# Block outputs formed transposed in PSUM, weight remainders by matmul, and another order of steps, in a fused linear-attention and mixture kernel on one core

## The chip, the cores and the metric

The kernel runs on one NeuronCore of a Trainium2 chip, as one launch. The core has five engines with queues of their own: TensorE (PE, with its weight loads PEld), VectorE (DVE), ScalarE (ACT), GpSimd (POOL) and SyncE (SP), whose queue issues all DMAs here. The metric is the device time of a run in microseconds; before the change it is 583.61 us, the median of 3 runs (582.99 to 583.75).

## What is computed

```python
for t in range(S):                       # B, H, S, D = 4, 8, 768, 48
    cur = einsum('bhd,bhe->bhde', u * k[t], v[t])
    y[t] = einsum('bhd,bhde->bhe', r[t], state + cur)
    state = w[t][..., None] * state + einsum('bhd,bhe->bhde', k[t], v[t])
x = y as 3072 tokens of 384              # heads side by side
h = x @ w_in; x = (h * cos(h)) @ w_out   # 384 -> 2048 -> 384, float64 weights
logits = x @ phi                         # 32 slots, 4 for each of 8 experts
slot_in = softmax(logits over tokens).T @ x
slot_out[e] = relu(slot_in[e] @ w1[e]) @ w2[e]     # 384 -> 1024 -> 384
out = softmax(logits over slots) @ slot_out
```

## The kernel before

**Attention.** The 3072 tokens are cut into 24 blocks of 128; a block is two chunks of 64 tokens, and heads go in four pairs. A block `j` is a series of short steps, each on one engine: the decays are transposed (`wT`, PE) and copied (`wf`, ACT); two running products are scanned on DVE (`scan` L153, `sp` L161); keys and receptances are transposed and scaled (`kT`, `ks`; `rT`, `L`); the scores of a chunk are formed (`A`) and masked, either on DVE straight from PSUM (`mask` L217) or by an ACT copy and a product on GpSimd (`mc`, `mp` L237), which the first seven blocks use; `U` gives what a chunk adds to the state; `z`, `st` carry the state on DVE and `rz` copies it, with ACT, into the tile `rz`, which already holds the chunk's values. `y` (L285) multiplies the tile `L` (scores and receptances) with `rz`: 16 products with 64 columns of `L` as weights and 48 columns of `rz` moving. The bonus of u is a product of r, u and k on GpSimd (`ru` L166, L167), a sum on DVE (`bo`) and a product with v on GpSimd (`bv` L257). `ya` (L295) adds it to `y` on DVE, from PSUM to SBUF; `xT` (L300) transposes the sum back into PSUM; `xh`, `xl` split it into two float32r parts, the left operand of the next stage.

**Weights.** w_in and w_out come as float64 words, in 8 pieces each, and are cut to float32 with integer operations: `abs` on ACT, then `mx`, `d1`, `d2a`, `d2b` on DVE. The list of steps has other ways for some pieces: `mxp` (the `mx` of L362 on GpSimd) and `d2s` with `d2p` (L383, L388: the shift on DVE, the addition on GpSimd). w_in is split in two float32r parts: `whi` on ACT and `wlo` (L402) on GpSimd. w_out stays float32; phi is multiplied into it by `oT`, `oc`, `om`, `pc`, `pT`, `ps` (L407 to L433).

**Feed-forward.** 12 groups of 256 tokens, each with 8 banks of 2 x 128 hidden columns. A half bank is 9 matmuls (`h`, L454 to L456); then come `turns` (ACT), `rest` (DVE L470), `cos` (ACT L474), `mul` (DVE L478), four transposes (`gT` L486) and a copy (`gc` L491). `l` (L499) takes logits, and `E` (L586) adds the group to the sums for the slots. Softmax statistics go with each group; all but the last use the Silu table, which lies in one set with Sin, the last uses Exp (`s_exp` L535), and the step `tab` loads that set.

**Tail.** When attention's memory is free, `att` loads six expert matrices of 1536 KB, `we` five more into places that w_in and the activations leave, and eight follow behind the last group and as experts are done; these are w1 in rows of 4096 B and w2 in rows of 1536 B (L669).

**Order.** Each engine runs its instructions in the order in which the program lists them, and `HEAD` (L897) is that list, written out: one word for a step, with its block, or group and bank. The transposes, scores and outputs of attention share one ring of three PSUM banks (`tps`).

Of the kernel before, what the change touches and what calls it, by code (L numbers as in the profile page):

```python
# [1055 lines left out]
```

## Time and profile before

| what | value |
|---|---|
| time, median of 3 runs | 583.61 us |
| span of the profiled execution | 579.7 us |
| PE busy | 507.9 us, 88% |
| DVE busy | 472.4 us, 81% |
| ACT busy | 312.8 us, 54% |
| POOL busy | 199.1 us, 34% |

The time of the profiled execution is known by its span, from its first instruction to its last; the 3.9 us to the median of the runs lie around it and are carried as they are. Busy times of engines overlap. A PE that is busy need not be at its peak, since the time of a matmul covers the start of the next ones; how many matmuls pass in a stretch tells more.

### The profile page before, as it was taken

The numbers are of one execution on the slowest core, as the hardware profiler recorded it, in microseconds if no ns is written. First come the engines' busy times: TensorE is split into PE (matmuls) and PEld (weight loads), VectorE is DVE, ScalarE is ACT, GpSimd is POOL, SyncE is SP. The second block draws the span as 40 slices with busy tenths as digits, with TensorE's granted clock in tenths as the row PEclk, the third lists the DMA queues.
The fourth block names the chain that finished last, engine by engine and source line by source line (L and its number), as shares of the span: only waits on it lengthen the run. The fifth ranks groups of instructions, "written<-read, shape, count | busy, mean of one in ns | idle before, by whom it ended". The sixth has DMA issues, their size and how long they took to land.

```text
span 579.7 us, 14183 instructions
## 1 busy us (share of the span) xinstructions
PE 507.9 (88%) x5778; PEld 436.1 (75%) x5778; DVE 472.4 (81%) x857; ACT 312.8 (54%) x655; POOL 199.1 (34%) x194
## 2 busy tenths in 40 slices
PE   2437968978999989999999999999989999998994
PEld 1335748767888969788888987897878979895663
DVE  5998999999898888798788899878979886657422
ACT  3334655665656465465565464654644756566421
POOL 5677865787241323241222231203221130000400
PEclk9957998799999999999999999999999999999997
DMA  9962764553241413330407232044032059568959
GB/s 239 254 168 63 165 163 97 111 135 58 56 83 29 83 29 55 57 69 7 90 19 106 45 63 51 13 71 84 1 63 36 16 218 355 191 218 263 377 176 277
DMA packets 150800, 67.39 MB, mean 116 GB/s; under 512 B 127568, under 2 KB 142928, under 8 KB 150736
## 3 DMA queue, kind: packets, MB, share of 16 engines
q1 hardware_dynamic: 150736, 66.49, 46.1%
q8 instruction: 46, 0.75, 0.6%
q14 instruction: 18, 0.15, 0.1%
HBM read 61.75 MB, written 4.72 MB: 115 GB/s over the span
## 4 chain that ended last, share of the span: by engine, by line
DVE 43%; PE 40%; ACT 7%; issue 5%; DMA 3%; SPq 0%; ACTq 0%; DVEq 0%
PE h L454 6%; PE h L456 6%; PE h L455 6%; DVE qt L153 5%; PE gT L486 4%; DVE pt L161 4%; DVE g L470 4%; DVE g L478 4%; DVE L L184 3%; DVE z L275 3%; DMA we<-in_moe_w_dram 3%; PE l L499 2%; ACT g L474 2%; DVE ao L373 2%; DVE L L224 2%
## 5 line engine op out<-in xcount | busy, mean ns | idle before, releaser
L454 PE MATMUL h<-x,wu 128*128 128x256 f32 x573 | 172.8, 301 | 0.1
L455 PE MATMUL h<-x,wu 128*128 128x256 f32 x573 | 162.5, 284 | 0.0
L456 PE MATMUL h<-x,wu 128*128 128x256 f32 x573 | 162.5, 284 | 0.0
L454 PEld LDWEIGHTS h<-x,wu 128*128 128x128 f32 x573 | 110.4, 193 | 1.0 <-PE wT L138 0.3
L455 PEld LDWEIGHTS h<-x,wu 128*128 128x128 f32 x573 | 110.7, 193 | 0.2
L456 PEld LDWEIGHTS h<-x,wu 128*128 128x128 f32 x573 | 110.3, 192 | 0.0
L474 ACT ACTIVATE g<-g,half_pi 128x512 f32<-128x512 f32 (+1 forms) x97 | 69.6, 718 | 68.1 <-DVE g L470 67.3
L466 ACT ACTIVATE g<-h 128x512 int32<-128x512 f32 x96 | 57.2, 596 | 51.2 <-PE h L456 43.5
L478 DVE TENSOR_TENSOR g<-g,h 128x512 f32<-128x512 f32 x96 | 65.0, 678 | 20.6 <-ACT g L474 19.9
L470 DVE SCALAR_TENSOR_TENSOR g<-g,h 128x512 f32<-128x512 int32 x96 | 64.9, 676 | 19.7 <-ACT g L466 16.7
L257 POOL TENSOR_TENSOR bv<-vz,bo 64x384 f32<-64x384 f32 x48 | 48.2, 1005 | 55.4 <-DVE bo L249 18.4
L491 ACT COPY gt<-gT 128x512 f32<-128x512 f32 x92 | 53.5, 583 | 24.4 <-PE gT L486 16.4
L486 PE MATMUL gT<-cs,g 128*128 128x128 f32 x384 | 59.5, 279 | 4.9 <-DVE g L478 4.8
L190 POOL MEMSET L<- 64x512 f32 x32 | 16.6, 519 | 111.4 <-PE y L291 78.9
L486 PEld LDWEIGHTS gT<-cs,g 128*128 128x128 f32 x384 | 43.3, 141 | 15.3 <-issue 6.1
L166 POOL TENSOR_TENSOR ru<-rn,u_b 128x384 f32<-128x384 f32 x24 | 27.7, 1153 | 72.6 <-DVE bo L249 36.5
L280 ACT COPY rz<-z 64x192 f32<-64x192 f32 x96 | 33.5, 349 | 25.1 <-DVE z L275 24.2
L291 PE MATMUL y<-rz,L 128*64 128x48 f32 x768 | 29.2, 231 | 12.9 <-DVE st_state L283 12.1
L291 PEld LDWEIGHTS y<-rz,L 128*64 128x64 f32 x768 | 26.3, 145 | 16.8 <-issue 14.1
L161 DVE TENSOR_TENSOR_SCAN pt<-wf,ini_f 128x520 f32<-128x520 f32 x24 | 35.3, 1473 | 0.3
L153 DVE TENSOR_TENSOR_SCAN qt<-wf,one_b 128x520 f32<-128x520 f32 x24 | 34.7, 1446 | 0.3
L499 PE MATMUL l<-g,p_sb 128*32 128x256 f32 x384 | 31.0, 393 | 3.6 <-DVE g L478 3.6
(180 smaller groups left out, 942.9 us busy)
## 6 DMA issues: line engine op xcount, KB each, us to landing
we<-in_moe_w_dram SPq DMA_DIRECT2D x16, 1536.0 KB, 9.7
rawi<-in_moe_w_in_dram SPq DMA_DIRECT2D x7, 768.0 KB, 4.8
wn<-in_w_dram SPq DMA_DIRECT2D x24, 192.0 KB, 3.5
kn<-in_k_dram SPq DMA_DIRECT2D x24, 192.0 KB, 4.2
rn<-in_r_dram SPq DMA_DIRECT2D x24, 192.0 KB, 3.6
vz<-in_v_dram SPq DMA_DIRECT2D x48, 96.0 KB, 3.3
rz<-in_v_dram SPq DMA_DIRECT2D x96, 48.0 KB, 2.5
out_dram<-ob SPq DMA_DIRECT2D x17, 256.0 KB, 3.8
```

Source lines behind the costliest of these rows:

```text
L153: nc.vector.tensor_tensor_scan(qt[:, n:0:-1], wf[:, n:0:-1], one_b[:, n:0:-1], 0.0, ALU.mult, ALU.add)
L161: nc.vector.tensor_tensor_scan(pt, wf[:, 0:NS * SEG], ini_f, 0.0, ALU.mult, ALU.add)
L291: nc.tensor.matmul(ps[64 * c:64 * c + 64, 2 * p + a, :], lhsT=L[:, a, 2 * p + c, :], rhs=rz[:, c, p, a, :], start=True, stop=True)
L454: nc.tensor.matmul(hp, lhsT=wh, rhs=xh[:, c, :], start=(c == 0), stop=False)
L455: nc.tensor.matmul(hp, lhsT=wh, rhs=xl[:, c, :], start=False, stop=False)
L456: nc.tensor.matmul(hp, lhsT=wl, rhs=xh[:, c, :], start=False, stop=(c == KD - 1))
L466: nc.scalar.activation(gt.bitcast(I32), hp, AF.Copy, bias=0.25, scale=1.0 / TWO_PI)
L470: nc.vector.scalar_tensor_tensor(out=gt, in0=gt.bitcast(I32), scalar=-TWO_PI, in1=hp, op0=ALU.mult, op1=ALU.add)
L474: nc.scalar.activation(gt, gt, AF.Sin, bias=half_pi[:, 0:1])
L478: nc.vector.tensor_tensor(out=gt, in0=gt, in1=hp, op=ALU.mult)
L486: nc.tensor.transpose(ps[:, tt, mm, :], gt[:, mm, tt * 128:(tt + 1) * 128], ident)
L491: (nc.vector.tensor_copy if NBK * g + i >= ATT and i in (1, 2) else nc.scalar.copy)(t, pend.pop(("gT", g, i)))
```

## The change

`y` is formed transposed. The new `e_y` uses 32 columns of `rz` as weights and 64 columns of `L` moving, 32 products for a block instead of 16, into the PSUM layout that `xT` had; `e_yb` adds the bonus to it with three transposing matmuls that accumulate. `ya`, the tile `y` and `xT` are gone. For this the tile of values is padded to 64 columns a head, in two fixed tiles (`rzs`) whose padding GpSimd writes once. The scores `A` of block 8 and later are formed with 64 moving columns instead of 128, and `mask` is two products instead of four. `mc` and `mp`, `mxp`, `d2s` and `d2p` are no longer in the list: all masks, all `mx` and all `d2b` are on DVE. `wlo` gives way to `wn`, two matmuls into PSUM (a times the identity, minus the rounded part times the identity), and `wc`, an ACT copy. `om` has w_out's tile as weights, so `pc` and `pT` go. w2 is loaded in rows of 3072 B, and a transpose in the tail reads every second column to fit. The list `HEAD` is another throughout.

```diff
+    neg = sm_p.tile([128, G], F32R, tag="lg", name="neg", bufs=1)[:, 0:128]      # -identity, by ACT at the start
+    rzs = [nat.tile([128, 2, HP, 2, 64], F32, name=f"rzs{i}") for i in range(2)]
+    RZ = (slice(0, D), slice(64 - D, 64))
...
     def e_A(j):
-        for s in range(NS if j >= WIDE else 0):
-            m, x = slice(64 * (s % 2), 64 * (s % 2) + 64), s - s % 2
-            nc.tensor.matmul(ps[m, x:x + 2, :], lhsT=ks[:, s, :], rhs=L[:, :, s, :], start=True, stop=True)
...
+        for s in range(NS):
+            for a in range(2):
+                k = slice(0, 128) if j >= WIDE else slice(64 * a, 64 * a + 64)
+                nc.tensor.matmul(ps[64 - 64 * a:128 - 64 * a, s, :], lhsT=ks[k, s, :], rhs=L[k, a, s, :], start=True, stop=True)
...
     def e_y(j):
-        for p in range(HP):
-            for a in range(2):
-                for c in range(2):
-                    nc.tensor.matmul(ps[64 * c:64 * c + 64, 2 * p + a, :], lhsT=L[:, a, 2 * p + c, :], rhs=rz[:, c, p, a, :],
-                                     start=True, stop=True)
+        for c in range(2):
+            for a, b in ((0, 0), (0, 1), (1, 0), (1, 1)):
+                for p in range(HP):
+                    o, m = divmod(32 * (3 * p + a + b), 128)
+                    nc.tensor.matmul(ps[m:m + 32, o, c * C:(c + 1) * C], lhsT=rz[:, c, p, a, 32 * b:32 * b + 32], rhs=L[:, a, 2 * p + c, :],
+                                     start=m not in begun, stop=False, skip_group_check=True)
+    def e_yb(j):
+        for c in range(KD):
+            nc.tensor.matmul(pend["xT", j][:, c, :], lhsT=y[:, c * 128:(c + 1) * 128], rhs=ident, is_transpose=True,
+                             start=False, stop=c == KD - 1, skip_group_check=True)
...
+    def e_wn(n, q):
+        nc.tensor.matmul(ps, lhsT=ident, rhs=a[:, k], start=True, stop=False)
+        nc.tensor.matmul(ps, lhsT=neg, rhs=hi[:, k], start=False, stop=True)
+    def e_wc(n, q):
+        nc.scalar.copy(win(n)[2][:, k], pend.pop(("wl", n, q)))
...
-            nc.tensor.matmul(pt_ps[u_][32 * q:32 * q + 32, 0:128], lhsT=phi_sb[:, c, :], rhs=wt_t[m][:, c, :], start=(c == 0), stop=(c == KD - 1))
+            nc.tensor.matmul(pt_ps[0][:, m, :], lhsT=wt_t[m][:, c, :], rhs=phi_sb[:, c, :], start=(c == 0), stop=(c == KD - 1))
...
-                src = w2[idx - NE].rearrange("(c p) f -> p c f", p=128)
+                src = w2[idx - NE].rearrange("(q p c) f -> p q (c f)", q=4, c=2)
```

What the other list does to the queues is seen in the programs' instructions. On DVE, in the first 40 us, where w_out's first pieces (`ao`, `rawo`) are cut: before,

```order
L364 TENSOR_SCALAR ao_249<-ao_249 128x768
L368 TENSOR_SCALAR ao_249<-ao_249 128x768
L273 MEMSET z_0_253 128x192
L373 SCALAR_TENSOR_TENSOR ao_249<-rawo_245,ao_249 128x768
L364 TENSOR_SCALAR ao_256<-ao_256 128x768
L249 TENSOR_REDUCE bo_264<-ru_261 128x8
L386 TENSOR_SCALAR rawo_245<-rawo_245 128x768
L368 TENSOR_SCALAR ao_256<-ao_256 128x768
L373 SCALAR_TENSOR_TENSOR ao_256<-rawo_245,ao_256 128x768
```

and now:

```order
L222 TENSOR_TENSOR L_218<-A_282,cs 64x512 x2
L277 TENSOR_TENSOR st_state<-U_264,z_1_299 128x192
L357 TENSOR_SCALAR ao_260<-ao_260 128x768
L361 TENSOR_SCALAR ao_260<-ao_260 128x768
L199 TENSOR_TENSOR ks_323<-kT_310,qt_197 128x512
L366 SCALAR_TENSOR_TENSOR ao_260<-rawo_238,ao_260 128x768
L374 SCALAR_TENSOR_TENSOR wo_sb<-rawo_238,ao_260 128x768
```

The mask of block 0 (L222) and the last cut (L374) are now DVE's own; the shift alone (L386) is gone.

On POOL, behind the first memsets (`ru` and `bv` are the bonus): before,

```order
L390 TENSOR_TENSOR ai_158<-rawi_152,ai_158 128x768
L404 TENSOR_TENSOR wu_194<-ai_158,wu_194 128x3x256
L404 TENSOR_TENSOR wu_242<-ai_163,wu_242 128x3x256
L166 TENSOR_TENSOR ru_261<-rn_119,u_b 128x384
L167 TENSOR_TENSOR ru_261<-ru_261,kn_121 128x384
L240 TENSOR_TENSOR L_216<-L_216,cs 64x512 x2
L390 TENSOR_TENSOR wo_sb<-rawo_245,ao_249 128x768
L257 TENSOR_TENSOR bv_316<-vz_125,bo_264 64x384 x2
```

and now:

```order
L169 TENSOR_TENSOR ru_240<-rn_117,u_b 128x384
L170 TENSOR_TENSOR ru_240<-ru_240,kn_119 128x384
L251 TENSOR_TENSOR bv_252<-vz_123,bo_250 64x384 x2
L169 TENSOR_TENSOR ru_479<-rn_118,u_b 128x384
L170 TENSOR_TENSOR ru_479<-ru_479,kn_120 128x384
L251 TENSOR_TENSOR bv_498<-vz_124,bo_482 64x384 x2
```

Only the bonus is left on POOL in this stretch.

On ACT, at the last group (`dl`, `al`: its exponentials; `gt`: its transposed activations; `dt`: what `E` needs): before,

```order
L686 ACT_TABLE_LOAD
L686 ACTIVATE half_pi<-half_pi 128x1
L491 COPY gt_5_6922<-gT_5_6885 128x512
L491 COPY gt_6_6937<-gT_6_6932 128x512
L533 COPY dl_115<-lc_6941 32x64 x4
L491 COPY gt_7_6957<-gT_7_6952 128x512
L543 ACTIVATE dl_115,sg_6968<-dl_115,nb_6946 128x64
```

and now:

```order
L530 COPY dl_112<-lc_7335 32x64 x4
L540 ACT_TABLE_LOAD
L540 ACTIVATE dl_112,sg_7362<-dl_112,nb_7340 128x64
L541 ACTIVATE al_7361<-dl_112,nb_7340 128x1
L575 COPY dt_7375<-dT_7373 64x64 x2
L488 COPY gt_7_7394<-gT_7_7352 128x512
L488 COPY gt_6_7396<-gT_6_7378 128x512
```

The load of the Exp set stood ahead of the copies and now stands right before the exponential; `tab` has moved to group 0, where the list now causes three table loads (one for Exp, one back to Sin, one for Silu).

## Rows read from the trace of the kernel before

**Rows 1.** The profile page: busy time; DVE's busy tenths in 40 slices of 14.5 us.
```profile
PE 507.9 (88%) x5778; PEld 436.1 (75%) x5778; DVE 472.4 (81%) x857; ACT 312.8 (54%) x655; POOL 199.1 (34%) x194
DVE  5998999999898888798788899878979886657422
```
**Rows 2.** Stages: start:end, length, busy us and instructions by engine, clock, DMA share, GB/s.
```profile
8.00:128.60 120.60, 84.57 (x867) 71.19 (x867) 117.89 (x145) 59.76 (x111) 86.46 (x52) 0.86 0.64 151
128.60:169.30 40.70, 38.23 (x439) 33.92 (x436) 37.47 (x57) 24.54 (x55) 23.50 (x18) 1.00 0.38 66
169.30:479.00 309.70, 295.82 (x3367) 259.12 (x3365) 266.22 (x542) 176.71 (x376) 78.20 (x94) 1.00 0.30 58
479.00:533.50 54.50, 52.85 (x522) 46.46 (x519) 33.66 (x77) 34.91 (x76) 0.82 (x1) 1.00 0.73 261
```
**Rows 3.** Waits of DVE, 0 to 128.6 us, the longest: us in total, times, longest.
```profile
DVE ai L364 <- ACT ai L360: 6.9, 1, 6.9
```
**Rows 4.** Groups of DVE instructions, 8 to 128.6 us: busy us, mean ns.
```profile
L153 DVE TENSOR_TENSOR_SCAN qt<-wf,one_b 128x520 f32<-128x520 f32 x7 | 13.0, 1860 | 0.0
L275 DVE TENSOR_TENSOR z<-st_state,qt 128x192 f32<-128x192 f32 x11 | 9.8, 893 | 0.1
L297 DVE TENSOR_TENSOR y<-y,bv 128x384 f32<-128x384 f32 x5 | 2.8, 551 | 0.8 <-PE y L291 0.8
```
**Rows 5.** DVE in order of time, 24 to 58 us: start, us.
```profile
26.02 1.50 DVE L368 TENSOR_SCALAR ao<-ao 128x768 int32<-128x768 int32 x1
30.32 0.55 DVE L386 TENSOR_SCALAR rawo<-rawo 128x768 int32<-128x768 int32 x1
51.64 0.34 DVE L275 TENSOR_TENSOR z<-st_state,qt 128x192 f32<-128x192 f32 x1
54.12 0.95 DVE L381 SCALAR_TENSOR_TENSOR ai<-rawi,ai 128x768 int32<-128x768 int32 x1
57.60 1.23 DVE L161 TENSOR_TENSOR_SCAN pt<-wf,ini_f 128x520 f32<-128x520 f32 x1
```
**Rows 6.** Groups of instructions of the whole run, shapes apart.
```profile
L228 DVE TENSOR_TENSOR L<-A,cs 64x512 f32<-64x512 f32 x2 | 1.4, 690 | 0.0
L224 DVE TENSOR_TENSOR L<-A,cs 64x256 f32<-64x256 f32 x64 | 27.0, 422 | 1.1
L686 ACT ACT_TABLE_LOAD x1 | 1.3, 1283 | 0.0
```
**Rows 7.** Groups of POOL instructions, 0 to 128.6 us, shapes apart: busy us, mean ns.
```profile
L240 POOL TENSOR_TENSOR L<-L,cs 64x512 f32<-64x512 f32 x12 | 19.5, 1624 | 1.9 <-ACT L L235 1.1
L404 POOL TENSOR_TENSOR wu<-ai,wu 128x768 fp32r<-128x768 f32 x8 | 15.8, 1983 | 13.3 <-ACT wu L400 13.3
L257 POOL TENSOR_TENSOR bv<-vz,bo 64x384 f32<-64x384 f32 x10 | 13.2, 1319 | 0.4
L166 POOL TENSOR_TENSOR ru<-rn,u_b 128x384 f32<-128x384 f32 x5 | 6.8, 1359 | 0.2
```
**Rows 8.** PE in order of time: start, us to the end of the last one, count.
```profile
201.52 0.28 PE L456 MATMUL h<-x,wu 128*128 128x256 f32 x1
...
202.16 1.14 PE L291 MATMUL y<-rz,L 128*64 128x48 f32 x32
203.23 0.64 PE L499 MATMUL l<-g,p_sb 128*32 128x256 f32 x8
...
210.57 1.09 PE L204 MATMUL A<-L,ks 128*64 128x128 f32 x16 [0.86 <-DVE st_state L283]
...
564.61 1.96 PE L824 MATMUL so<-we,wo_sb 128*32 128x128 f32 x64
```
**Rows 9.** The chain that ended last: the tail's DMA.
```profile
542.03 15.30 DMA we<-in_moe_w_dram
```
**Rows 10.** Two stretches in which only expert matrices load: w1, then w2.
```profile
482.00:494.00 12.00, 12.00 (x110) 11.28 (x110) 7.06 (x17) 6.82 (x14) 0.00 (x0) 1.00 1.02 410
535.00:554.00 19.00, 18.99 (x336) 11.65 (x340) 7.53 (x20) 7.43 (x20) 5.86 (x9) 1.00 1.06 375
```

More of the change, by code (lines that the diff above doesn't have):

```diff
@@ L649, in rwkv_moe_kernel @@
                 nc.gpsimd.memset(t[64 * c:64 * c + 64, :, 1 - c, :], 0.0)
+        for t in rzs:
+            for a in range(2):
+                nc.gpsimd.memset(t[:, :, :, a, 48 - 48 * a:64 - 48 * a], 0.0)
         nc.gpsimd.memset(ini_f, 0.0)
@@ L906 @@
-bo.2 d2b.i.4 wT.3 wf.3 scan.3 bv.2 om.5 oT.7 oc.7 rT.2 L.2 whi.4 lk.3 ru.3 sr.3 om.6 kN.2 om.7 abs.i.3 mx.i.3 wT.4 h.0.0.1 wlo.4
-ksn.2 turns.0.0 sp.3 wf.4 d1.i.3 rest.0.0 kT.3 A.2 ks.3 h.0.1.0 mc.2 mp.2 U.2 d2a.i.3 d2s.i.3 lk.4 kN.3 raw.i.6 lz.2 lw.5 lk.5 lv.3
-rT.3 st.2.0 cos.0.0 mul.0.0 d2p.i.3 z.2.1 abs.i.6 mx.i.6 st.2.1 d1.i.6 d2s.i.6 rz.2.1 d2a.i.6 h.0.1.1 turns.0.1 rest.0.1 rz.2.0
-ksn.3 gT.0.0 h.0.2.0 h.0.2.1 gc.0.0 turns.0.2 whi.3 cos.0.1 pc.1 L.3 y.2 ya.2 z.3.0 scan.4 kT.4 d2p.i.6 whi.6 mul.0.1 wlo.3 lr.5
@@ L910 @@
-lv.4 A.3 mc.3 ks.4 wlo.6 U.3 st.3.0 rest.0.2 z.3.1 bo.3 sr.4 l.0.1 raw.i.5 abs.i.5 st.3.1 raw.i.7 cos.0.2 mul.0.2 sp.4 kN.4 ksn.4
-abs.i.7 mx.i.7 h.0.3.0 h.0.3.1 pT.1 gT.0.2 xT.2 gc.0.2 ps.1 xh.2 mxp.i.5 d1.i.5 lr.4 lz.3 rz.3.0 rz.3.1 d2s.i.7 d2a.i.5 xl.2
-h.0.4.0 rT.4 wT.5 wf.5 gT.0.1 d2b.i.5 mp.3 whi.5 L.4 h.0.4.1 d1.i.7 turns.0.3 rest.0.3 d2a.i.7 lw.6 bv.3 y.3 ya.3 A.4 lz.4 raw.o.4
-wlo.5 d2p.i.7 lw.7 gc.0.1 cos.0.3 z.4.0 mul.0.3 ru.4 raw.o.5 mc.4 U.4 scan.5 st.4.0 turns.0.4 rest.0.4 abs.o.4 sr.5 kT.5 z.4.1 wT.6
@@ L914 @@
-gT.0.3 whi.7 wlo.7 h.0.5.0 h.0.5.1 sp.5 cos.0.4 st.4.1 ks.5 l.0.3 rT.5 mul.0.4 wf.6 turns.0.5 rest.0.5 L.5 kN.5 xT.3 gc.0.3 lv.5
-ksn.5 cos.0.5 gT.0.4 h.0.6.0 mul.0.5 bo.4 scan.6 mxp.o.4 d1.o.4 h.0.6.1 abs.o.5 gc.0.4 xh.3 turns.0.6 xl.3 d2a.o.4 mxp.o.5 d1.o.5
-rz.4.0 rz.4.1 gT.0.5 A.5 gc.0.5 h.0.7.0 h.0.7.1 mc.5 d2b.o.4 oT.9 oT.8 turns.0.7 mp.4 y.4 oc.9 oc.8 d2a.o.5 rest.0.6 cos.0.6 lk.6
-lz.5 d2b.o.5 om.8 om.9 oT.11 bv.4 ya.4 oc.11 mul.0.6 oT.10 oc.10 lr.6 sr.6 mp.5 rest.0.7 cos.0.7 z.5.0 U.5 st.5.0 z.5.1 sp.6 st.5.1
@@ new lines @@
+turns.0.2 wc.1.1 mul.0.0 gT.0.0 om.4 lk.3 kT.3 mask.2 z.2.1 st.2.1 scan.3 ks.3 rest.0.2 whi.4 abs.i.3 mx.i.3 d1.i.3 sr.3 d2a.i.3
+d2b.i.3 sp.3 wn.4.0 kN.3 ksn.3 wn.4.1 h.0.1.0 h.0.1.1 wc.4.0 lw.5 raw.i.6 abs.i.6 lv.4 whi.3 gc.0.0 lk.4 mx.i.6 cos.0.2 wc.4.1
+wn.3.0 oT.7 wc.3.0 rT.3 wn.3.1 raw.i.5 d1.i.6 rz.2.1 oc.7 y.2 wc.3.1 d2a.i.6 turns.0.1 abs.i.5 mul.0.2 L.3 A.3 wT.4 h.0.3.0
+d2b.i.6 wf.4 mx.i.5 d1.i.5 z.3.0 whi.6 mask.3 wn.6.1 ps.0 wc.6.1 rest.0.1 scan.4 yb.2 om.5 cos.0.1 xh.2 kT.4 d2a.i.5 ru.3 lk.5
@@ new lines @@
+st.4.0 z.4.1 st.4.1 rz.4.1 d2b.o.4 y.3 mul.0.4 l.0.3 A.4 yb.3 xh.3 kT.5 ks.5 mask.4 h.0.5.0 xl.3 h.0.5.1 lw.6 lk.6 raw.o.6 rT.5
+mx.o.5 lz.5 d1.o.5 turns.0.5 kN.5 ksn.5 sr.5 rest.0.5 oT.8 gT.0.3 oc.8 oT.9 sp.5 d2a.o.5 gc.0.3 bo.4 oc.9 d2b.o.5 cos.0.5 h.0.7.0
+h.0.7.1 lv.5 bv.5 turns.0.7 wT.6 om.9 wf.6 mul.0.5 gT.0.5 rest.0.7 L.5 oT.11 raw.o.7 U.5 A.5 oc.11 om.11 z.5.0 scan.6 st.5.0
+abs.o.6 mx.o.6 z.5.1 lw.7 abs.o.7 d1.o.6 d2a.o.6 st.5.1 rz.5.1 om.8 cos.0.7 z.6.0 d2b.o.6 mul.0.7 h.0.6.0 h.0.6.1 wT.7 oT.10
@@ new lines @@
+h.1.1.0 h.1.1.1 mask.5 tab turns.0.6 gc.0.5 rest.0.6 gT.0.4 kT.6 cos.0.6 oc.10 sr.6 sp.6 mul.0.6 ks.6 oT.13 oc.13 rz.5.0 om.10
+gc.0.4 ps.2 wf.7 rT.6 mx.o.7 d1.o.7 h.1.0.0 oT.12 oc.12 d2a.o.7 d2b.o.7 close l.0.5 om.13 oT.14 oT.15 om.12 turns.1.1 bv.4 ru.6
+oc.14 oc.15 h.1.0.1 scan.7 om.15 om.14 gT.0.6 rest.1.1 y.5 lz.7 turns.1.0 cos.1.1 rest.1.0 mul.1.1 cos.1.0 mul.1.0 L.6 y.4 ps.3
+l.0.7 A.6 gc.0.6 sum.0 lc.0 sr.7 gT.0.7 h.1.2.0 h.1.2.1 max.0 exp.0 lv.6 mask.6 lw.9 turns.1.2 gc.0.7 xt.0 rest.1.2 cos.1.2
@@ new lines @@
+h.1.7.1 h.2.1.0 h.2.1.1 dc.0 turns.1.7 rest.1.7 A.7 scan.8 U.7 sr.8 sp.8 st.7.0 z.7.1 st.7.1 l.1.5 y.6 cos.1.7 mul.1.7 E.0.0
+rz.7.0 l.1.7 wT.9 gc.1.5 turns.2.1 rest.2.1 cos.2.1 rz.7.1 gT.1.4 gc.1.4 mask.7 zl.8 bv.7 mul.2.1 h.2.0.0 h.2.0.1 turns.2.0 kT.8
+gT.2.1 rest.2.0 cos.2.0 mul.2.0 E.0.1 yb.6 es.0 bo.8 wf.9 gc.2.1 h.2.3.0 rT.8 gT.1.6 L.8 lz.8 ks.8 h.2.3.1 turns.2.3 rest.2.3
+cos.2.3 sum.1 scan.9 h.2.2.0 sr.9 mul.2.3 xh.6 gc.1.6 xl.6 h.2.2.1 y.7 l.2.1 gT.1.7 yb.7 turns.2.2 rest.2.2 kN.8 lc.1 max.1 xh.7
@@ new lines @@
+y.8 turns.2.6 rest.2.6 ks.10 mul.2.7 bv.8 zl.10 E.1.0 E.1.1 cos.2.6 mul.2.6 gc.2.5 l.2.5 l.2.7 sum.2 gT.2.4 es.1 yb.8 rT.10 sp.10
+lk.12 L.10 h.3.1.0 h.3.1.1 turns.3.1 st.9.0 z.9.1 rz.9.1 bo.9 rest.3.1 gc.2.4 lw.11 xh.8 cos.3.1 xl.8 h.3.0.0 lv.10 mul.3.1
+h.3.0.1 A.10 lc.2 wT.11 st.9.1 turns.3.0 rest.3.0 lw.13 mask.10 cos.3.0 mul.3.0 gT.2.6 gc.2.6 max.2 exp.2 xt.2 xr.2 kN.10 h.3.2.0
+h.3.2.1 gT.3.1 lz.10 h.3.3.0 h.3.3.1 l.3.1 gc.3.1 turns.3.2 rest.3.2 wf.11 scan.11 ksn.10 cos.3.2 mul.3.2 y.9 turns.3.3 xd.2
@@ new lines @@
+lv.13 l.3.5 cos.3.7 mul.3.7 ks.12 rz.10.1 y.10 bv.10 gT.3.5 mask.11 cmb.0.2 h.4.0.0 h.4.0.1 bo.12 rest.3.6 gc.3.5 cos.3.6
+turns.4.0 st.11.0 z.11.1 rz.11.1 gT.3.4 rT.12 yb.10 lk.13 xh.10 st.11.1 mul.3.6 rest.4.0 lz.12 lv.12 sp.12 zl.12 gc.3.4 cos.4.0
+h.4.1.0 h.4.1.1 gT.3.7 wT.13 gc.3.7 mul.4.0 h.4.2.0 es.2 L.12 h.4.2.1 xl.10 l.3.7 turns.4.1 rest.4.1 cos.4.1 turns.4.2 cmb.0.3
+mul.4.1 A.12 wf.13 gT.3.6 gc.3.6 sum.3 rest.4.2 cos.4.2 rz.11.0 kN.12 h.4.3.0 ksn.12 mul.4.2 lc.3 scan.13 max.3 gT.4.1 gc.4.1
```

249 lines of the change are left out of this document (110 added, 139 removed).

## The prediction

> **What bounds the kernel now.** I read the page first, then a table of stages, then the waits and groups of the stage that stood out. The page has PE at 88% and DVE at 81%, and its slices show DVE nearly full in the first tenth to quarter of the run [rows 1]. The stages separate the two. The first matmul of group 1 starts at 128.6 us; from 8 us to there DVE is busy 117.9 of 120.6 us and PE only 84.6. From 128.6 to 533.5 us, when the last `E` ends, PE is busy 38.2 + 295.8 + 52.9 = 386.9 of 404.9 us and DVE 337.4 [rows 2]. So DVE sets the end of the head and PE that of the long middle. In the head DVE waits for nothing worth having: 6.9 us for its first piece of w_in [rows 3], and twice 0.8 us.
>
> DVE's head is not all work. There a scan takes 1.86 us on average and `z` 0.89 us [rows 4]; where GpSimd runs nothing beside them the same instructions take 1.23 and 0.34 us, and a simple operation on 768 columns takes 0.55 us instead of 1.50 [rows 5]. Counting every DVE group of the head in that way, mean less the undisturbed time, gives 32 us of stretching: the scans 7 x 0.63 = 4.4, `z` 11 x 0.55 = 6.0, the weight operations and the other scan the rest. GpSimd is busy 86.5 us of that stage [rows 2].
>
> **The head, up to group 1.** I counted the steps ahead of the first bank of group 1 in both lists. DVE gains five masks from PSUM, 2 x 0.69 us each [rows 6]: +6.9; six `d2b` at 0.95 [rows 5]: +5.7; seven `mx` at 0.55: +3.9; one `d1` and one `d2a` of a piece that now comes sooner: +1.5. It loses five `d2s` at 0.55 and five `ya` at 0.55 [rows 4, 5]: -5.5; and one `sp`, one `ks` and one bank's `rest` and `mul` fall behind the mark, less a `bo` and a `z`: -2.6. The net is +9.9 us, from 96 to 106 us undisturbed.
>
> GpSimd loses `mp`, `wlo`, `mxp` and `d2p`, of which the first two alone are 35 us [rows 7]. What stays is six `ru` and five `bv`, 12 instructions of 1.36 and 10 of 1.32 us, 29 us at these prices [rows 7], a third of 86.5; undisturbed they would be about 20 us, a quarter. So the stretching falls from 32 to between 7 and 11 us; I take 9. DVE's sum changes by 9.9 - 23 = -13.1 us. Neighbouring instructions overlap a little (128 us of durations make 118 busy), so this is worth 12.2 us of time. Against it: the remainders of w_in now go PE, ACT, PE through the ring of three banks in which attention's transposes queue, and a table load of 1.28 us [rows 6] stands on ACT twice in group 0, with a third after it. Behind each wait the banks' `cos` and attention's copies. ACT is half idle there [rows 2], so I give back 2 us of a possible 0 to 12. Head: **-10.2 us**.
>
> PE's new work in the head is hidden by DVE: a remainder is two plain matmuls and one float32r matmul's worth of columns. From 256 columns at 0.21 us plain and 0.12 us float32r [rows 8], 512 + 256 columns, the plain ones in two passes, cost 1.6 us, 13 us for 8 pieces. If that cover were gone they would all count. `om` trades 128 moving columns for 128 weight columns: I take nothing, between -6 us and 0. The `wc` copies (16, some 7 us) take the place of the `mc` copies, 6 x 1.16 us.
>
> **The middle, where PE counts.** The output `y` is the term to settle. Each float32 product is two matmuls in the trace, so `y` is 32 now and 64 after. 32 take 1.14 us with a last one of 0.22: 0.029 us each, 0.059 for a pair on two column halves [rows 8]. Where columns bound, a pair of 128 columns (`A`) takes 0.109 and four of 128 (`so`) take 0.107 us [rows 8], 0.85 ns a column whatever the number of tiles. 48 columns would be 0.041, so `y` is held by something else, which fits its weights, 128 columns a pair. After the change four matmuls have 64 moving and again 128 weight columns. The price of four is 0.054 us if columns bind, 0.059 if weights do as now, and 0.107 if no four go faster than the fastest four in the trace. I take 0.059, from the nearest row: 16 x 0.059 = 0.94 us a block, as now. `yb` is three transposes, as `xT` was.
>
> `A` of block 8 and later goes from 8 pairs at 0.109 to 16 at 0.059: about -0.09 us for 16 blocks, -1.4 us. `pT` goes, -0.5. With 13 added, PE's sum grows by 10.9 us, 9.6 of it ahead of the mark. That leaves +1.3 us behind it. Steps I price at 390 us on PE now take 404.9 us there, a ratio of 1.04, so **+1.4 us**. DVE has 15 us less to do there, 19 `ya` and 64 masks of 0.42 turned into 32 of 0.69 [rows 4, 6]; PE binds, so I count 1 us of it, between 0 and 9: **-1 us**.
>
> **The tail.** The Exp table was loaded beside other work; now its 1.28 us [rows 6] stand between the last group's copies and its exponential, and `E` follows: +1.2. The second half of that `E` waits for two copies behind `dt` instead of one: +0.4. The last five expert matrices, 7.9 MB, are in flight from about 533 us and PE waits 15.3 us for the last of them [rows 9]; they flow at 375 GB/s in rows of 1536 B, while w1 came at 410 in rows of 4096 B [rows 10]. Rows of 3072 B lie between: -1.8 to 0, I take -1.7. Tail: **-0.1 us**.
>
> Sum: -10.2 + 1.4 - 1 - 0.1 = -9.9 us. It is made on the profiled span of 579.7 us, giving 569.8; the 3.9 us around the span stay, so the median of 583.6 becomes **573.7 us**.
>
> **Rivals.**
>
> *Narrow matmuls bind (slower).* At 0.107 us for four, `y` costs 1.71 us, +0.77 a block. 20 blocks have their `y` behind the mark, where PE counts: +15.4 us, 589 us with nothing absorbed, some 586 with PE's idle 4% taking some. It decides from 0.09 us for four on, where 20 x 16 x 0.031 us eats the 9.9. For it: no row sustains less than 0.027 us a matmul, and the change asks for 0.015. Against it: at 0.027 the `so` row is explained by its columns alone. The Trainium skill, "TensorE: Matmul & The Clock Gate", Part 1 (the section on 56 ns against 53.3 ns), says that matmuls never start less than about 25 ns apart, however few the columns; by that rule a block's `y` is 1.6 us and the result near 587. The trace respects that figure on average and does not test it, as it has no shorter matmuls on four tiles.
>
> *The head's gain is given back.* DVE takes over work that nothing has to fetch from GpSimd, but each mask now waits on PE, and `y`'s PSUM bank is held until `bv` has come and `xl` is done, with two banks left for the rest. If the waits replace the stretching, the change does not do what it can: 12 us of gain gone is 584, half gone is 578. For it: DVE had only 1.6 us of such waits in the head, so the order was loose where this one may not be. Against it: masks and `d2b` sit several instructions behind their sources in the new queue.
>
> *PE closes up.* PE is idle 18 us in the middle. If fewer DVE steps there bring back half, the result is 565. Against it: most of DVE's waits there are on ACT's part of a bank, which does not change.
>
> **From cases to numbers.** The forecast, 566 to 580, has 0.53; narrow matmuls 0.17, mostly slower; the gain given back 0.18, half of it still faster, the rest about even; PE closing up 0.12. Within 0.2% (1.2 us) is about what a measurement of this kernel can tell from no change. That makes 0.74 faster, 0.06 the same, 0.20 slower. The range takes the forecast, most of PE's case and most of the narrow one: 563 to 587.
>
> **What would show it.** Right: group 1's first `h` near 118 us in the profile, not 128.6; scans near 1.3 us in the head and POOL busy near 25 us there; `y` at about 1 us for 64 matmuls; the stretch from that `h` to the last `E` near 405 us; the wait for w2 with over 390 GB/s. Wrong: a `y` of 1.7 us is the first rival; DVE idle by over 10 us in the head, on PE or ACT, is the second; under 396 us in the middle the third. A table load on the chain in the tail would confirm that term, and one in group 0 that delays DVE would correct my 2 us.

## The result and the profile after

The changed kernel takes 565.54 us, the median of 4 runs (562.68 to 567.16); the kernel before took 583.3 us beside it (581.6 to 583.75). The ratio is 0.970, 95% interval [0.967, 0.973]: 17.8 us faster, where 9.9 were forecast. Its profiled execution is the slowest of the four: 567.16 us, with a span of 565.4. In all executions on record whose time and span are both known the time is 1.7 to 2.1 us above the span, so the 3.9 us that the forecast carried do not all lie around it: 579.7 us is the span of one of the shorter executions of the kernel before, of some 581.6 us. The two profiles are therefore 14.3 us apart and not 17.8.

The busy line, DVE's slices and the shares of the chain that ended last, from the page of the changed kernel:

```profile
PE 516.0 (91%) x6846; PEld 447.6 (79%) x6846; DVE 438.7 (78%) x823; ACT 313.3 (55%) x657; POOL 123.2 (22%) x163
DVE  4998997996778888788887799897897596666413
PE 58%; DVE 27%; ACT 6%; DMA 4%; issue 3%; SPq 0%; DVEq 0%; ACTq 0%
```

The same last line on the page of the kernel before:

```profile
DVE 43%; PE 40%; ACT 7%; issue 5%; DMA 3%; SPq 0%; ACTq 0%; DVEq 0%
```

DVE is less full at the start than in [rows 1], and the chain has passed from DVE to PE. The stages, cut at the same events as in [rows 2] (group 1's first `h` at 123.0 us, group 2's at 161.4, the last `E` ending at 520.5; columns as there):

```profile
8.00:123.00 115.00, 91.67 (x986) 75.57 (x986) 103.37 (x157) 60.02 (x113) 28.82 (x26) 0.91 0.69 157
123.00:161.40 38.40, 38.18 (x463) 35.39 (x464) 28.52 (x50) 25.46 (x52) 4.59 (x5) 0.96 0.38 63
123.00:520.50 397.50, 386.68 (x5263) 345.85 (x5263) 317.24 (x625) 236.18 (x506) 83.69 (x103) 1.00 0.37 88
520.50:565.40 44.90, 36.61 (x594) 25.48 (x594) 16.05 (x38) 14.19 (x34) 5.86 (x9) 0.95 0.81 282
```

| stage | before | after | moved | forecast |
|---|---|---|---|---|
| head, to group 1's first `h` | 128.6 | 123.0 | -5.6 | -10.2 |
| middle, to the end of the last `E` | 404.9 | 397.5 | -7.4 | +2.0 (the middle's +0.4, the tail's +1.6 ahead of `E`) |
| behind it | 46.2 | 44.9 | -1.3 | -1.7 |

In the head DVE is busy 103.4 us instead of 117.9, a little less than the 105.7 that follow from the forecast, but it now idles 11.6 us instead of 2.7. In the middle PE is as busy as before (386.7 against 386.9 us), and its idle time fell from 18.0 to 10.8 us. DVE is busy 20.1 us less there.

Two groups of DVE answer to [rows 4], in the head (busy us, mean ns):

```profile
L156 DVE TENSOR_TENSOR_SCAN qt<-wf,one_b 128x520 f32<-128x520 f32 x6 | 8.9, 1480 | 1.1 <-ACT wf L151 1.1
L269 DVE TENSOR_TENSOR z<-st_state,qt 128x192 f32<-128x192 f32 x11 | 6.2, 561 | 0.2
```

The scan fell from 1.86 to 1.48 us, `z` from 0.89 to 0.56: most of the stretching went with GpSimd's work (28.8 us in the head instead of 86.5), not all. What DVE waits for in the head now, in place of [rows 3] (us in total, times, longest):

```profile
DVE g L467 <- ACT g L463: 2.8, 2, 2.1
DVE x L313 <- ACT x L309: 2.0, 2, 1.8
DVE st_state L277 <- PE U L259: 1.9, 2, 1.1
DVE qt L156 <- ACT wf L151: 1.1, 1, 1.1
DVE ao L357 <- ACT ao L353: 1.0, 1, 1.0
```

And PE and ACT in order of time, at a block's output and scores and at the last exponential:

```profile
200.84 1.10 PE L288 MATMUL y<-L,rzs 128*32 128x64 f32 x64 [0.39 <-DVE L L222]
...
210.12 1.15 PE L208 MATMUL A<-L,ks 128*64 128x64 f32 x32
...
515.70 1.28 ACT L540 ACT_TABLE_LOAD   x1
517.00 0.35 ACT L540 ACTIVATE dl<-dl,nb 128x64 f32<-128x64 f32 x1
```

For `y`, 64 matmuls (32 columns of weights, 64 moving) take 1.10 us, as 32 (64 of weights, 48 moving) took 1.14. For the scores, 32 with 64 moving columns take 1.15 us where 16 with 128 took 1.09 [rows 8]. The table load stands on the way to the last `E`.

### The profile page after: what moved, and what is told of

Read it like the earlier page. It is cut to its first block, busy times and chain, and to the rows that moved or that the text cites. A ratio compares the mean times of both kernels' runs of the same rounds, so it can differ in the third digit from the quotient of the medians.

```text
span 565.4 us, 16220 instructions
## 1 busy us (share of the span) xinstructions
PE 516.0 (91%) x6846; PEld 447.6 (79%) x6846; DVE 438.7 (78%) x823; ACT 313.3 (55%) x657; POOL 123.2 (22%) x163
## 3 DMA queue, kind: packets, MB, share of 16 engines
q1 hardware_dynamic: 146640, 66.49, 46.6%
## 4 chain that ended last, share of the span: by engine, by line
PE 58%; DVE 27%; ACT 6%; DMA 4%; issue 3%; SPq 0%; DVEq 0%; ACTq 0%
PE h L451 9%; PE h L453 8%; PE h L452 8%; PE gT L483 5%; PE l L496 3%; PE y L288 3%; PE E L592 3%; DVE g L475 3%; DMA we<-in_moe_w_dram 3%; PE A L208 3%; DVE L L222 3%; DVE g L467 3%; DVE L L187 2%; PE U L259 2%; DVE qt L156 2%
## 5 line engine op out<-in xcount | busy, mean ns | idle before, releaser
L251 POOL TENSOR_TENSOR bv<-vz,bo 64x384 f32<-64x384 f32 x48 | 41.9, 873 | 151.8 <-DVE bo L243 56.6
L274 ACT COPY rzs<-z 64x192 f32<-64x192 f32 x96 | 33.4, 348 | 9.5 <-DVE z L269 8.4
L156 DVE TENSOR_TENSOR_SCAN qt<-wf,one_b 128x520 f32<-128x520 f32 x24 | 31.9, 1329 | 6.5 <-ACT wf L151 6.4
L187 DVE TENSOR_TENSOR L<-rT,pt 64x512 f32<-64x512 f32 x48 | 32.9, 686 | 4.3 <-PE y L288 2.8
L222 DVE TENSOR_TENSOR L<-A,cs 64x512 f32<-64x512 f32 x48 | 33.1, 689 | 1.2
L496 PE MATMUL l<-g,p_sb 128*32 128x256 f32 x384 | 29.8, 385 | 1.5 <-DVE g L475 1.5
L164 DVE TENSOR_TENSOR_SCAN pt<-wf,ini_f 128x520 f32<-128x520 f32 x24 | 30.2, 1258 | 0.2
```

The costliest lines, as they stand in the source:

```text
L187: nc.vector.tensor_tensor(out=L[h, a], in0=ps[h], in1=segs(pt, 0, C)[h], op=ALU.mult)
L222: nc.vector.tensor_tensor(out=L[h, a], in0=ps[h], in1=mask[h].unsqueeze(1).to_broadcast([64, NS, C]), op=ALU.mult)
L496: nc.tensor.matmul(lps_t[g][32 * mm:32 * mm + 32, 0:G], lhsT=p_sb[:, m, :], rhs=g_t[g, m // 2][:, m % 2, :], start=(m < 4), stop=(m >= MF ...
```

## The experiments

All stages below come from profiles, cut at the same three events. "Mark" is group 1's first `h`. Times are medians; the kernel before has 582.5 to 583.4 us beside them.

| kernel | time | mark | middle | tail | PE busy, middle | DVE busy, middle |
|---|---|---|---|---|---|---|
| before | 583.3 | 128.6 | 404.9 | 46.2 | 386.9 | 337.4 |
| changed | 565.5 | 123.0 | 397.5 | 44.9 | 386.7 | 317.2 |
| changed, again | 565.0 | 120.7 | 395.5 | 44.8 | 385.3 | 315.4 |
| GpSimd's products back | 591.2 | 149.5 | 395.5 | 44.7 | 384.9 | 313.0 |
| remainders on GpSimd | 583.9 | 139.2 | 395.9 | 46.0 | 385.3 | 315.2 |
| old output | 598.0 | 125.7 | 425.0 | 45.0 | 396.0 | 325.7 |
| before, products on DVE | 585.1 | 135.8 | 402.5 | 46.4 | 386.6 | 335.0 |
| before, new output | 588.4 | 129.4 | 412.3 | 45.3 | 390.0 | 328.8 |
| 40 reductions more on DVE | 573.1 | 121.6 | 405.4 | 44.6 | 390.4 | 334.5 |
| `tab` late | 563.0 | 122.0 | 394.5 | 45.0 | 384.9 | 315.2 |
| before, DVE with less to do | 575.7 | 129.7 | 397.3 | 46.9 | 385.4 | 317.9 |
| remainders by one matmul | 565.3 | 122.1 | 397.6 | 46.1 | 386.8 | 316.1 |
| `y` twice | 586.3 | 120.1 | 418.0 | 44.7 | 404.6 | 316.8 |
| old scores, old w2 rows | 571.0 | 121.5 | 403.8 | 46.6 | 388.9 | 321.3 |

**The changed kernel again.** No edit.

> The changed kernel again, unaltered, to learn how far its time and its stage marks scatter. Every theory expects 565.5 us within 2, group 1's first h at 123 us and the last E ending near 520 us, each within 1.5. If the marks scatter by more than that, no theory can be told from another by one profile.

Ratio 0.969 [0.967, 0.972]. The mark came 2.3 us sooner and the last `E` ended 4.3 us sooner than in the first profile, more than I had allowed. The mark lies between 120.1 and 123.0 us in the seven profiles whose head is the changed kernel's but for the remainders' matmul or loads, and the middle between 395.5 and 397.6, mean 396.4, in the five where next to nothing behind the mark differs. Smaller differences than these say nothing.

The two longer middles of the five (397.5 and 397.6 us) have a short stretch right behind the mark in which PE was granted 0.50 of its clock, 1.2 GHz; the three others (395.5 to 395.9) keep 2.4 GHz there. The first profile of the changed kernel and the second:

```profile
124.20:127.20 3.00, 3.00 (x16) 3.00 (x15) 2.70 (x5) 1.58 (x3) 0.00 (x0) 0.50 0.00 0
```
```profile
121.20:124.20 3.00, 3.00 (x28) 2.92 (x27) 2.95 (x6) 2.28 (x3) 0.00 (x0) 1.00 0.00 0
```

In both PE was busy 1.8 of the 4 us before the mark, so the same work leads to either.

**GpSimd's products back in the new list.**

```diff
-mask.j            (j < 7)      mx.x.n (8 pieces)    d2b.x.n (5 pieces)
+mc.j mp.j                      mxp.x.n              d2s.x.n d2p.x.n
```

> The changed kernel with GpSimd's products of before back in the same places of the new list: seven masks as an ACT copy and a GpSimd product, eight maxima and five additions of the shifted words on GpSimd. Ahead of group 1 DVE loses five masks (6.9 us), seven maxima (3.9) and 5 x 0.4 for the shifts (2.0), 12.8 us of undisturbed work. Theory 1, contention as I priced it (these three kinds stretched DVE by 14.6 us ahead of the mark before): DVE's busy time in the head goes from 103 to about 105 us and the mark from 123 to about 125, the time to 567 or more. Rival A, the price of contention was wrong and only DVE's own work counts: DVE busy about 91 us in the head, mark near 112, time near 555. Rival B, the head is now set by waits of PE and ACT and no longer by DVE: mark within 1 us of 123 whatever DVE does.

Ratio 1.014 [1.011, 1.017], and none of the three. The head, and DVE's waits in it:

```profile
8.00:149.50 141.50, 103.83 (x987) 86.02 (x987) 100.87 (x142) 67.12 (x125) 68.34 (x48) 0.78 0.57 127
```
```profile
DVE bo L243 <- POOL ru L170: 8.7, 2, 5.5
DVE ao L361 <- POOL ao L357: 7.4, 3, 4.0
DVE g L467 <- ACT g L463: 7.0, 2, 4.1
DVE ai L361 <- POOL ai L357: 5.8, 2, 4.2
```

DVE's busy time is 100.9 us. Without 12.8 us of work (11.8 of busy time at my 0.92) the second profile's 102.7 would be 90.9, so 10 us of stretching came back, of the 13 that I had priced. Compared group by group with the second profile, the instructions that both have took 10.0 us longer too: contention is real and about that large. But DVE idles 40.6 us, 21.9 of them behind GpSimd in these rows. In a list that counts on DVE's 0.55 us for a maximum, a GpSimd step is a link in a chain, and these waits cost more than the contention. PE's clock was lower as well, 0.78 over this head where the changed kernel has 0.91 and 0.94; its share of the delay was not separated.

**Remainders of w_in on GpSimd.**

```diff
-wn.n.0 wn.n.1 wc.n.0 wc.n.1
+wlo.n             (right behind whi.n)
```

> The changed kernel with the remainder of w_in taken by GpSimd again (one subtraction a piece behind its rounding) in place of two matmuls and two ACT copies. PE loses 8 x 1.6 to 2.1 us, ACT some 7 us; GpSimd gains 16 us, which stretched DVE by 8.1 us before. Theory 1, DVE with its stretching sets the head: DVE busy 111 us there, mark at 129 to 131, time 572. Rival B, the remainders on PE, which stand on the chain of the new kernel at half clock with 2 us each, and their three banks of PSUM set the head now: DVE's idle time of 11.6 us shrinks by the same as its busy time grows or more, mark between 117 and 124, time 560 to 566.

Ratio 1.000 [0.998, 1.003], so this alone takes back the whole gain. DVE is busy 111.0 us in the head, as theory 1 said, 8.4 more than in the second profile; but its idle time doubled too, from 10.0 to 20.2 us (131.2 - 111.0), and the mark is at 139.2 instead of 130. Rival B falls. Of the idle time, 6.4 us are waits for `U`, and PE waits for a load of v ahead of a `U`:

```profile
DVE st_state L277 <- PE U L259: 6.4, 2, 5.3
```
```profile
PE U L259 <- DMA vz<-in_v_dram: 7.8, 1, 7.8
```

So part of the loss is a late load, and why it came late stays open; the clock was 0.79 in this head. The 8.4 us are contention: the same groups of DVE took 8.4 us longer.

**The old output in the new list.**

```diff
-yb.j        y.j: 64 matmuls, rzs as weights
+ya.j xT.j   y.j: 32 matmuls, L as weights, 48 columns; ya adds in place of bv
```

> The changed kernel with the block output as before: 48 columns of values moving against 64 columns of weights, the bonus added on DVE from PSUM (in place of the bonus tile), and three transposes. PE's own work stays (0.94 us a block for y in both), DVE gains 24 x 0.55 us, 10.5 us of it behind group 1's first h. Theory M1, the middle became shorter because DVE has less to do there and PE waits less: the middle grows by 4 to 8 us, PE idle in it from 10.8 to 15 or more, time 570 to 575. Rival M3, the middle became shorter because the list is better ordered: the middle grows by under 1.5 us and the time stays under 568. In the head, 5 x 0.55 us of DVE's work come back on top: 0 to 2.6 us.

Ratio 1.025 [1.022, 1.028]. The middle grew by 29 us, far beyond both theories. PE's waits there:

```profile
PE xT L296 <- DVE bv L290: 20.2, 13, 4.0
PE h L450 <- DVE g L474: 2.5, 3, 1.4
```

The list puts `yb` close behind `y`, since nothing but PE stands between them. With DVE's sum there again, PE stops at 13 transposes, 20.2 us in all. PE's busy time rose by 10 us too, with a clock of 0.98 over this middle (1.00 in the changed kernel's). In the old list the same wait cost 1.1 us. The run prices the hand-over in a list that isn't made for it, not the value of the change of form.

**The kernel before with GpSimd's products on DVE.**

```diff
-mc.j ... mp.j     mxp.x.n    d2s.x.n ... d2p.x.n
+mask.j            mx.x.n     d2b.x.n               (at the place of GpSimd's step)
```

> The kernel before, its list otherwise as it was, with the seven masks, eight maxima and five last cuts that GpSimd shared done by DVE alone, at the places of GpSimd's steps (the seven ACT copies and five shifts go too). Up to group 1 DVE gains 12.8 us of undisturbed work and, by my prices, loses 13.6 to 14.6 us of stretching. Theory 1: DVE busy in the head between 115 and 118 us (117.9 before), the mark at 126 to 129, time 581 to 584; so the change of engine alone brings little, and what the changed kernel gained in the head came from the remainders of w_in and from the list. Rival D, GpSimd's products disturb less than I priced: DVE busy 125 us or more, mark at 135, time 590. Rival L, in the old list too GpSimd's steps stand in chains (13 to 28 us when put back into the new list): mark at 120 or earlier, time under 576.

Ratio 1.004 [1.002, 1.005]: slightly slower. The head:

```profile
8.00:135.80 127.80, 89.40 (x867) 74.58 (x867) 117.06 (x164) 53.43 (x100) 47.88 (x30) 0.81 0.65 146
```

DVE's busy time is 117.1 us beside 117.9 before [rows 2]: 12.8 us more work and as much less stretching, as theory 1 has it. Its idle time rose from 2.7 to 10.7 us, 4.5 of them in one wait for ACT's `turns`, and the mark came 7.2 us later. So the exchange is even in DVE's time, and the waits decide.

**The kernel before with the new output, blocks 6 to 23.**

```diff
-y.j ... ya.j ... xT.j ... xh.j ... xl.j
+y.j ... yb.j (in ya's place)  xh.j (3 steps on)  xl.j (7 steps on)
```

> The kernel before with the transposed output alone, for blocks 6 to 23: 64 narrow matmuls, the bonus added by three matmuls at the place where DVE added it, the ACT copy and the DVE difference three and seven steps behind it, all else in its list as it was. DVE loses 18 x 0.55 = 9.9 us in the middle and each block uses one PSUM bank of the ring less. Theory M1, less work and one hand-over fewer between PE and DVE shorten the middle: 404.9 us before, 397 to 402 here, time 576 to 581. Rival M3, the old list had the hand-overs covered (PE waited 1.1 us in all for DVE's sums) and only a new list can use the freedom: 403 to 406 us, time 582 to 585. Rival N, 64 narrow matmuls are dearer than 32 with 48 columns: over 408 us.

Ratio 1.008 [1.006, 1.011]; the middle grew by 7.4 us to 412.3, which is rival N's number. But PE's work grew only by 3.1 us, and the price of `y` is settled below; PE's idle time went from 18.0 to 22.3, 3.8 of it in one wait of `U` for a load of v, and DVE waits 7.2 us for `U` there. My placing of `xh` and `xl` may have brought that; no run tried another. So the run doesn't price the new form. It does show that 8.6 us less of DVE's work need not shorten a middle whose order was changed as well.

**40 reductions more on DVE.**

```diff
+    dm_t = nat.tile([128, H], F32, name="dm")
+    def e_dm(j):
+        nc.vector.tensor_reduce(out=dm_t, in_=u_b, axis=AX.X, op=ALU.add)
-xl.j
+xl.j dm.j dm.j    (j >= 4)
```

> The changed kernel with 40 reductions of 128x384 on DVE added (0.54 us each, two behind each block's difference from block 4 on, their result used by nothing): 21.6 us of DVE's time, what the change took from DVE in the middle (337 to 317 us). Theory M1, PE closed up because DVE has less to do: the middle grows by 6 to 8 us (395.5 to 402 or more), time 571 or more. Rival M3, PE's idle time went by the order of the list and DVE has slack to spare (it is idle 80 us in the middle): the middle grows by under 2 us, time 565 to 567.

Ratio 0.983 [0.980, 0.986]. The middle, and the added group:

```profile
121.60:527.00 405.40, 390.43 (x5263) 347.52 (x5263) 334.51 (x665) 236.13 (x506) 83.51 (x103) 0.99 0.36 86
```
```profile
L302 DVE TENSOR_REDUCE dm<-u_b 128x8 f32<-128x384 f32 x40 | 21.9, 547 | 0.7
```

405.4 us, 9.0 above the mean of the five: 0.41 us for each us of the reductions, though DVE idles 71 us there, nothing waits for the reductions themselves and PE is busy 96%. This middle has two short stretches at 0.50 of the clock, one right behind the mark and one from 368.5 us, behind a wait of PE. Beside the two of the five that have the first as well the growth is 7.8 us, 0.36 for each; the medians of the runs, 573.1 and 565.0, say 0.37. M1 holds, M3 falls.

**The Exp table late.**

```diff
-mask.5 tab turns.0.6 ... cos.11.7.1 E.10.0
+mask.5 turns.0.6     ... cos.11.7.1 tab E.10.0
```

> The changed kernel with the step that loads the Exp table where it was before, behind the last cosine of the last group, and not in group 0: one load instead of four behind the first. The load of 1.28 us leaves the chain of the last exponential: the last E ends 1.0 to 1.4 us sooner after group 11's first h, and if ACT's three loads in group 0 (3.8 us) delayed the head, the mark of group 1 or 2 comes up to 3 us sooner. My terms give 1.2 us for the tail and some 1 us for group 0: time 562 to 564. Rival: ACT waits there for other things and covers the loads: no difference, 565.

Ratio 0.966 [0.962, 0.969], 563.0 us: the fastest kernel here, though its interval overlaps that of the changed kernel. ACT in order of time:

```profile
509.11 1.28 ACT L688 ACT_TABLE_LOAD   x1
...
512.17 0.84 ACT L530 COPY dl<-lc 32x64 f32<-32x64 f32 x4 [0.26 <-DVE mx L519]
513.05 0.35 ACT L540 ACTIVATE dl<-dl,nb 128x64 f32<-128x64 f32 x1
```

From group 11's first `h` to the end of the last `E` it takes 35.9 us; both profiles of the changed kernel have 37.2. So the load on the chain costs 1.3 us. The mark stays in its range: the three loads of group 0 cost the head nothing that shows.

**The kernel before, DVE with less to do.**

```diff
 e_ya:  n = 1 if j >= 4 else H      # heads that the sum takes, in place of bv
 b_mul: gt, hp = gt[:, 0:1], hp[:, 0:1]   # where mm is None, g >= 1 and i odd
```

> The kernel before with the same instructions in the same order on every engine and less to do in some of DVE's: the sum of output and bonus takes 48 of 384 columns from block 4 on (0.55 to about 0.15 us, 19 of them behind group 1's first h), and the last product of every second bank from group 1 on takes one of its two halves (0.68 to about 0.40 us, 44 of them). Left out is most of the output of attention and half of those products. DVE loses some 8 + 12 = 20 us in the middle. Theory M1, DVE's work in the middle decides about half of it even where PE is busy 96% (40 added reductions cost the changed kernel 9.9 us of its middle, 0.46 us for each us): the middle falls from 404.9 by 7 to 10 us to 395 to 398, time 574 to 577. Rival M3, PE bound the old middle and its idle time was in the order of the list: 403 us or more, time 581 or more.

Ratio 0.989 [0.985, 0.993].

```profile
129.70:527.00 397.30, 385.38 (x4320) 339.55 (x4318) 317.92 (x673) 235.93 (x507) 102.14 (x113) 1.00 0.38 88
```

DVE lost 19.4 us in the middle and the middle 7.6, 0.39 for each, with the old list and the old forms of everything; by the medians of the runs it is 6.8 us, 0.35 for each. Neither this middle nor that of the kernel before has a stretch at half clock. That is the size of what the change gained there (20.1 us of DVE, 7.4 of time).

**Remainders by one matmul.**

```diff
-        nc.tensor.matmul(ps, lhsT=ident, rhs=a[:, k], start=True, stop=False)
-        nc.tensor.matmul(ps, lhsT=neg, rhs=hi[:, k], start=False, stop=True)
+        nc.tensor.matmul(ps, lhsT=neg, rhs=hi[:, k], start=True, stop=True)
```

> The changed kernel with one of the two matmuls of a remainder: the plain float32 one, a times the identity, is left out (so the remainder is only minus the rounded part). PE loses 6144 columns in two passes, 10 to 13 us at the full clock and more at half, all ahead of group 1; every step, wait and bank stays. Theory 1, DVE sets the head and the waits that came back (DVE idle 2.7 us before, 11 us now) are on hand-overs: the mark stays within 1.5 us of 121 to 123. Rival P, PE's new work stands on the head's chain (one remainder took 2 us there at half clock) and took back what DVE gained: the mark comes 3 to 10 us sooner, DVE idle in the head falls to 5 us or less, time 556 to 562.

Ratio 0.969 [0.965, 0.972].

```profile
8.00:122.10 114.10, 87.26 (x954) 76.09 (x954) 102.51 (x156) 59.99 (x113) 29.11 (x26) 0.84 0.72 157
```

Mark, DVE's idle time and the median of the runs are unchanged; rival P's gain did not come. The profile is a weaker test than meant: its clock in the head was 0.84 instead of 0.91 to 0.94, and PE's busy time fell by 3 to 4 us instead of 10. It is the one execution of four with so low a clock (0.958 over the span, the others 0.972 to 0.977), so the missing matmul need not be the reason.

**`y` twice.**

```diff
-        for c in range(2):
+        for c in range(4 if j >= 4 else 2):     # then c % 2, starting anew at c = 2
```

> The changed kernel with the 64 narrow matmuls of a block's output issued twice from block 4 on, the second time over the first. My price of 0.94 us a block and the trace's 1.10 us for 64 in a row put 19 to 20 us of PE's time into the middle. Theory: PE binds there, every us of it counts: the middle grows by 18 to 21 us, time 583 to 586. Rival: PE's idle 10 us take some of it: 9 to 16 us, time 574 to 581. By the floor of about 25 ns for each matmul it would be 30 us and more, time above 594.

Ratio 1.005 [1.003, 1.008].

```profile
120.10:538.10 418.00, 404.60 (x6543) 363.63 (x6543) 316.77 (x625) 236.32 (x506) 83.47 (x103) 1.00 0.35 84
```

1280 more matmuls put 18.8 us on PE and 21.6 on the middle (against the means of the five, 385.8 and 396.4): 15 to 17 ns for each, 0.94 to 1.08 us a block. PE's work counts in full, and the price of 0.94 holds.

**Old scores and old rows of w2.**

```diff
 e_A, j >= 8:    one matmul of 128 moving columns for each head, as before
 e_mask, j >= 8: four products of 64x256, as before
-src = w2[idx - NE].rearrange("(q p c) f -> p q (c f)", q=4, c=2)
+src = w2[idx - NE].rearrange("(c p) f -> p c f", p=128)
```

> The changed kernel with two separate parts as before, read at different stages: from block 8 on the scores with 128 moving columns and four mask products of 0.42 us instead of two of 0.69 (DVE +0.3 us a block, 16 blocks), and w2 in rows of 1536 B with contiguous columns in the tail's transposes. My terms: PE +1.4 us and DVE +4.8 us, which at 0.46 us for each is 2.2, so the middle grows by 2 to 4 us; the tail behind the last E grows by 1.7 us (44.8 to 46.5), time 568 to 570. Rival for the tail: the wait for w2 is set by the place where its DMAs are issued, not by the length of its rows: 44.8 stays. Rival for the middle: one matmul of 128 columns costs less than two of 64, so that it shrinks.

Ratio 0.979 [0.975, 0.983]. The waits for w2 in the tail, of this kernel and of the changed one run again:

```profile
533.50 17.24 DMA we<-in_moe_w_dram
```
```profile
524.32 15.42 DMA we<-in_moe_w_dram
```

The wait is 1.8 us longer (it is 15.2 to 15.7 us where the other kernels with the new rows have it on this chain), and the tail 46.6 us: in this order of loads the rows of w2 are worth the 1.7 that I took. The 15.30 us of the kernel before [rows 9] belong to another order, and beside them the changed kernel's wait of 15.46 us is no shorter. The middle grew by 7.4 us in this profile (its run is the slowest of four, 573.7) and by some 4 in the median, 571.0 - 565.3 - 1.7. The scores' matmuls are not the reason: my +1.4 us had the wrong sign, and in the old form they take 17.3 us from block 8 on, in the new one 18.5. PE's busy time rose by 3.1 us all the same, with three short stretches at 0.50 of the clock (from 122.7, 368.4 and 522.0 us) that the second profile doesn't have. DVE's 5.9 us more, at the 0.4 below, are 2.4; the rest of the 4 is not explained, and four runs from 568.3 to 573.7 us leave room for it.

## Why the prediction was right in sign and short in size

- **The step that failed** is, in the middle, "PE binds, so I count 1 us of it, between 0 and 9: -1 us". DVE's relief there is worth about 0.4 us for each us: 0.36 to 0.41 by adding work to the changed kernel, 0.35 to 0.39 by taking work out of the kernel before. The relief was also 20.1 us and not 15, since group 1's stage lost its GpSimd products as well (POOL 23.5 us busy there before [rows 2], 4.6 after; the groups of DVE that both kernels have there took 4.8 us less). 0.4 x 20.1 = 8.0 us, and 7.4 and 9.4 were measured in the two profiles, of which the first has the stretch at half clock. A PE that is busy 96% isn't alone in setting the time. The chain of the kernel before said so, with 43% on DVE over the run and 36% added up over the middle alone, and so did PE's waits in its middle, of which these are the largest; neither went into my sum.

```profile
PE gT L486 <- DVE g L478: 2.9, 5, 0.8
PE woT L410 <- DVE wo_sb L381: 2.3, 2, 1.8
PE U L265 <- DVE bo L249: 2.2, 1, 2.2
```

- **The rival that came true** is "PE closes up", with 565 us, to which I gave 0.12. Its mechanism is what was seen: PE's idle time in the middle fell by 7.2 us where it said 9. That its number came out as well is in part luck: in the two profiles of the changed kernel the head gave 4.6 and 2.3 us less than my sum, and the middle 1.4 and 3.4 more than this rival's -6 (+2.0 with -9 in place of -1).
- **The head** was right in DVE's work and wrong in what came back. DVE fell to 103.4 and 102.7 us where I had 105.7, and the prices of contention held on three kernels (10 of 13 us, 8.4 of 8.1, and an even exchange in the old list). I gave back 2 us for waits; 9 came back in the first profile, 7 in the second, so the rival "the gain is given back" took a good half of its 12. They are spread over hand-overs from ACT and PE; neither PE's remainders nor the table loads were seen to cause them, though the test of the remainders was weak, and which of them could be removed stays open.
- **The output `y`**: 0.94 us a block was right, and "narrow matmuls bind" fell. The Trainium skill, "TensorE: Matmul & The Clock Gate", Part 1, has no two matmuls start less than about 25 ns apart. Here 64 on four column tiles of 32 take 1.10 us, some 14 ns each with the last one's 0.22 us taken off, so this trace disagrees, at least for matmuls on different tiles.
- **The scores**: my -1.4 us for `A` doesn't follow from my own prices. 8 pairs at 0.109 are 0.87 us and 16 at 0.059 are 0.94, so it should have been +1.2 us for 16 blocks, and the forecast a gain of some 7 us. The traces have 17.5 us before and 18.5 after. What the new form gives comes from its masks, 5 us less for DVE, which I left inside DVE's 1 us; both put back cost some 4 us.
- **The tail**: the Exp load costs 1.3 us (1.2 forecast). Undone alone, w2's rows cost 1.7 to 1.8 us (1.7), but the tail of the changed kernel did not gain that much from them: from the end of the last `E` to the last matmul it takes 37.4 us, 37.7 before. Another 1.0 of the 1.3 us lies behind the last matmul, where the profiles of both kernels' variants take either some 7.5 or some 8.5 us, so that 1.0 isn't shown to be the change's. The 0.4 us for the second half of the last `E` was not tried alone.
- **The parts** can't be added up: three of them undone alone cost 19 to 33 us, more than the whole change gains, and two put alone into the old list made it slower. Each list is laid out for its own forms. How much of the gain is the list's, and how much the forms', is not separated by these runs; the relief of DVE is the one part that both lists value alike.

## What to carry to other kernels

Don't read "busy 96%" as "the other engines are free": add and remove a known amount of work on the second engine, and take its price from the stage (here about 0.4 us for each us). When work moves off an engine that is slow to answer, count its contention and the hand-overs on both sides of it; in a hand-written order the hand-overs can be the larger part. And to judge one part of a change by undoing it in a list made for the whole overstates it. Before two profiles are compared stage by stage, see where each lies among the runs of its kernel and where its clock fell.
